# Transposing the normalised rows of twelve of sixteen x tiles with the DMA crossbar in place of TensorE

## The chip, the cores and the metric

The kernel runs on one core of one Trainium2 chip. The metric is the time of one execution on the device in microseconds; the median of several runs is compared. A profile is one further execution, taken by the hardware profiler.

## The reference, cut to what matters

```python
def reference(A_x, A_w_r, A_w_i, B_x, B_w_in, B_w_sp, B_b_sp, B_w_out):   # S = 2048, D = 576, Fh = 2304
    xn = layernorm(A_x)                      # over D
    s = irfft2(rfft2(xn) * (w_r + 1j * w_i)) # 2-D Fourier filter over S and D
    z = gelu(xn @ w_in)                      # D -> 2 Fh
    z1, z2 = z[..., :Fh], layernorm(z[..., Fh:])
    g = w_sp @ z2 + b_sp[:, None]            # mixes along S
    g = silu((z1 * g) @ w_out)
    return A_x + s * g
```

Everything that multiplies xn on TensorE, the first Fourier step along D and both halves of xn @ w_in, needs xn with D on the partitions: a transpose of each 128 rows.

## The kernel before

The 2048 rows are 16 tiles of 128 (MT = 16). A normalised row is laid out as KS = 5 blocks of 128 columns: four blocks of D, and a fifth that holds the 64 columns left over twice, so that the upper and the lower half of the partitions can each feed a half-height matmul.

**The first stage**, which the change touches, goes over the tiles. For tile m:

- ln1(m): VectorE takes mean and variance (L270, L274), GpSimd the reciprocal root (L261, L263).
- ln1_apply(m), L289: two VectorE operations (L293, L296) write the normalised row into XN[m % 3], one of three buffers.
- xpose(m), L300: five TensorE transposes into a PSUM tile pt of the pool psh (L304), and one ScalarE copy (L305) into xnT[:, m], which keeps all sixteen transposed tiles.
- p0_fold(m), L309: VectorE makes sums and differences of mirrored blocks (L311, L312) into one of four buffers FS.
- p0(m), L324, and p0_tail(m), L316: the first Fourier product, eight matmuls of 128 x 290 out of FS and two half-height ones out of the fifth block of xnT.
- p0_out(m), L332: ScalarE copies the product to bf16 (L334), GpSimd's queue stores it into the DRAM tensor Ad (L336).

In between, fill(1) emits a chunk of xn @ w_in: four full matmuls and a half-height one of 128 x 384 (L458), with GELU on ScalarE (L477). For the first 32 chunks these are of the second half of w_in.

The order is written out by hand: inside manual_schedule (L740) the queues of SP, TensorE and VectorE run in the order of the source; ScalarE and GpSimd are ordered by the framework's scheduler. Tiles 0, 1 and the start are written singly; the loop at L781 goes over m = 2 to 15. An even pass emits xpose(m + 1), p0_fold(m), ln1(m + 3), ln1_apply(m + 2), a chunk, p0(m), a chunk with the half-height matmuls of tiles m and m + 1 (p0_pair, L752). An odd pass emits p0_fold(m), ln1(m + 3), ln1_apply(m + 2), p0(m), p0_out(m), a chunk, xpose(m + 1), a chunk. So tile m + 2 is normalised in pass m and folded in pass m + 2.

SP's queue, in its order, first carries x (in four pieces), w_in for the second half, constants (CDSD, then G1, 1 MB, as c_g at L257), then MM (c_mm, L780), then the first two groups of w_in for the other half: load_win1 (L242), called in the passes m = 6 and m = 9 and made of two large loads (L232) and four small ones (L236). Each SP DMA completes on one of eight semaphores in turn, and waits until the DMA eight places ahead of it has completed on the same one. No SP DMA of this stretch waits for an engine, so they are issued as early as these waits allow, ahead of the passes in which they stand in the source.

After the loop: eleven chunks, then the further Fourier steps through DRAM (Ad, Bd, Ed, Yd) mixed with the rest of the chunks (to about 210 us), and then the product with w_sp, the gate and w_out (L617, L671). The slabs of w_sp are loaded with DMA transposes from DRAM on SP (L534).

Of the kernel before, what the change touches and what calls it, by code (L numbers as in the profile page):

```python
# [90 lines left out]
def kernel(  # L91
# [12 lines left out]
    nc = tc.nc  # L104
# [4 lines left out]
    MT = S // P  # L109
    KS = (D + P - 1) // P  # L110
# [57 lines left out]
    def reg(name, off, n):  # L168
        return AR[:, offs[name] + off: offs[name] + off + n]
# [15 lines left out]
    XN = [reg("XN", i * KS * P, KS * P) for i in range(3)]  # L185
# [7 lines left out]
    xnT = reg("XT", 0, MT * KS * P).rearrange("p (m k t) -> p m k t", m=MT, k=KS)  # L193
# [48 lines left out]
    def load_win1(g):  # L242
        fs = slice((g % (FT // WG)) * WG * P, (g % (FT // WG) + 1) * WG * P)
        wb = WIN1[g % 2]
        load_win(wb, fs)
# [36 lines left out]
    def ln1(m):  # L282
        ln1_stats(m)
        ln1_aggr(m)
# [4 lines left out]
    def ln1_apply(m):  # L289
        xn = XN[m % 3]  # L290
        mean, rs = ln1_of[m]
        xr = XC[m // 4][:, m % 4, :].rearrange("p (a d) -> p a d", a=2)
        nc.vector.tensor_scalar(out=xn[:, 0:4 * P].rearrange("p (b a i) -> p a b i", b=2, a=2),  # L293
                                in0=xr[:, :, 0:2 * P].rearrange("p a (b i) -> p a b i", b=2), scalar1=mean, scalar2=rs,
                                op0=ALU.subtract, op1=ALU.mult)
        nc.vector.tensor_scalar(out=xn[:, 4 * P:KS * P].rearrange("p (r a i) -> p r a i", r=2, a=2),  # L296
                                in0=xr[:, None, :, 2 * P:H2].to_broadcast((P, 2, 2, HT)), scalar1=mean, scalar2=rs,
                                op0=ALU.subtract, op1=ALU.mult)

    def xpose(m):  # L300
        xn = XN[m % 3]
        pt = psh.tile([P, KS, P], BF16, tag="h")
        for ks in range(KS):
            nc.tensor.transpose(pt[:, ks, :], xn[:, ks * P:(ks + 1) * P], ident[:])  # L304
        nc.scalar.activation(out=xnT[:, m, :, :], in_=pt[:], func=ACT.Identity)  # L305
# [3 lines left out]
    def p0_fold(m):  # L309
        xe, xo = xnT[:, m, 0:KS - 1:2, :], xnT[:, m, 1:KS - 1:2, :]  # L310
        nc.vector.tensor_tensor(out=FS[m % 4][:, 0, :, :], in0=xe, in1=xo, op=ALU.add)  # L311
        nc.vector.tensor_tensor(out=FS[m % 4][:, 1, :, :], in0=xe, in1=xo, op=ALU.subtract)  # L312
# [11 lines left out]
    def p0(m, start):  # L324
        if start:
            p0_ps[m] = psa.tile([P, 2, 512], F32, tag="a", name="pa")
        for par in range(2):
            for k in range(2):
                nc.tensor.matmul(p0_ps[m][:, par, 0:2 * LE], lhsT=FS[m % 4][:, par, k, :], rhs=CDSD[:, par, k, :],  # L329
                                 start=start and k == 0, stop=not start and k == 1, skip_group_check=True)  # L330

    def p0_out(m):  # L332
        sg = PST[m % 8].rearrange("p (c l) -> p c l", c=2)
        nc.scalar.activation(out=sg.rearrange("p c (l a) -> p a c l", a=2),  # L334
                             in_=p0_ps[m][:, :, 0:2 * LE].rearrange("p a (c l) -> p a c l", c=2), func=ACT.Identity)
        nc.gpsimd.dma_start(out=Adw[m], in_=sg[:, :, 0:L])  # L336
# [175 lines left out]
    def spend(pe, dve=0.0):  # L512
        load["pe"] += pe
        if dve:
            load["dve"] = max(load["dve"], load["pe"]) + dve
# [193 lines left out]
    def fill(n, lead=1.2, tails=None, ahead=None):  # L709
        for _ in range(n):  # L710
            i = place[0]
            place[0] += 1
            if i % 4 < 2:
                held.append(chunk(i))
                full(held[-1], True)
            if i % 4 == 1:
                if ahead:
                    ahead()
                done = held[:]
                held[:] = [chunk(i + 1), chunk(i + 2)]  # L720
                assert not tails or n == 1
                for r, c in enumerate(sorted(done + held, key=lambda c: c.wide)):
                    c.mm(KS - 1, slice(r % 2 * KT, (r % 2 + 1) * KT), c in held, c in done)
                if tails:
                    tails()
            elif i % 4 >= 2:
                done = [held.pop(0)]
                full(done[0], False)
            else:
                done = []  # L730
            for c in done:
                if c.wide == ZC:
                    z1_store(None, None)
                tick[0] += 1
                c.post()
            spend(0.82 if kinds[i] == "2" else 1.07)
            z2_stats(lead)

    SP, PE, DVE = mybir.EngineType.SP, mybir.EngineType.PE, mybir.EngineType.DVE
    with tc.manual_schedule(engines={SP, PE, DVE}):  # L740
# [11 lines left out]
        def p0_pair(m):  # L752
            p0_tail(m, False)
            p0_tail(m + 1, True)
            p0_out(m)

        ln1(0)
        ln1_stats(1, (0,))
        nc.vector.reciprocal(out=ln1_of[0][1], in_=ln1_of[0][1])
        ln1_apply(0)  # L760
        nc.scalar.activation(out=THF[:, 0:1], in_=ln1_of[0][1], func=ACT.Gelu_apprx_tanh)
        xpose(0)
# [3 lines left out]
        fill(1, 0)  # L766
        ln1(2)
        ln1_apply(1)
        p0_fold(0)
        ln1_apply(2)  # L770
        ln1(3)
        fill(1, 0, lambda: p0_pair(0), lambda: (xpose(1), p0(0, True), xpose(2)))
# [6 lines left out]
        fill(1, 0)  # L779
        nc.sync.dma_start(out=MM, in_=cd_mm.ap().rearrange("p (a k) -> p a k", a=3))  # L780
        for m in range(2, MT):  # L781
            if m % 2 == 0:
                xpose(m + 1)
            spend(0.78, 2.35 if m + 3 < MT else 0.6)
            p0_fold(m)
            if m + 3 < MT:
                ln1(m + 3)
            if m + 2 < MT:
                ln1_apply(m + 2)
            if m % 2 == 0:  # L790
                fill(1, 0)
                p0(m, True)
                fill(1, 0, lambda: p0_pair(m))
            else:
                p0(m, False)
                p0_out(m)
                fill(1, 0)
                if m + 1 < MT:
                    xpose(m + 1)
                fill(1, 0)  # L800
            if m in (6, 9):
                load_win1(m // 9)
# [119 lines left out]
```

## Time and profile before

| | us |
|---|---|
| median of 3 runs (lowest, highest) | 502.13 (502.05, 502.26) |
| the profiled execution, own time | 501.63 |
| its span | 499.9 |
| TensorE busy | 489.2 |
| VectorE busy | 342.6 |
| ScalarE busy | 169.4 |
| GpSimd busy | 210.8 |

The page's part 1 gives the busy time of each engine; PE is TensorE's matmuls, PEld its weight loads, DVE VectorE, ACT ScalarE, POOL GpSimd, SP the engine that only issues DMAs (its queue is SPq). The granted TensorE clock was 1.00 over the execution. A chain of waits is followed back from the last instruction to what released it; a timeline lists instructions with start, duration, engine, line, operation, tiles written and read, and in brackets the idle time before and what ended it. DMA issues list size and the median time from issue to landing. AR is one large SBUF tile that holds nearly all buffers, so XN, xnT, FS and the weights all appear under that name and are told apart by line and shape.

### The profile page before, as it was taken

The page shows a single profiled execution, that of the slowest core. Times are in us where ns is not written, and L with a number is a line of the kernel's source. Part 1 is how long each engine was busy: PE and PEld are TensorE (multiplying, and loading weights), DVE is VectorE, ACT ScalarE, POOL GpSimd, SP SyncE. Part 2 cuts the span into 40 slices and gives each one's busy share as a digit, 9 for nine tenths or more (in the row PEclk, how much of TensorE's full clock was granted, in tenths as well). Part 3 has the DMA queues.
Part 4 walks back from the last instruction along what each step waited for, and adds up shares of the span by engine and source line. Part 5 has one row for each costly group of instructions (what it writes and reads, how often), then busy time and mean ns, then how long its engine had stood idle before and what let it go on. Part 6 is the DMA issues. An engine that isn't in the chain of part 4 may idle for free.

```text
span 499.9 us, 9370 instructions
## 1 busy us (share of the span) xinstructions
PE 489.2 (98%) x3454; PEld 308.6 (62%) x3454; DVE 342.6 (69%) x746; ACT 169.4 (34%) x355; POOL 210.8 (42%) x281
## 2 busy tenths in 40 slices
PE   7999999999999999899999999999999999999996
PEld 2655454555556544466666677666666678888885
DVE  5776588898656798966565648856656547877734
ACT  4878777686778556200000011000000011000001
POOL 2664324434242684644535501455354301666600
PEclk9999999999999999999999999999999999999999
DMA  7951688988362999772112599021111863111202
GB/s 244 352 160 49 229 284 250 329 223 229 122 242 87 243 245 251 198 244 64 33 33 63 121 158 229 25 63 33 47 49 33 173 136 94 51 48 45 79 26 71
DMA packets 86766, 70.67 MB, mean 141 GB/s; under 512 B 39776, under 2 KB 79328, under 8 KB 86464
## 3 DMA queue, kind: packets, MB, share of 16 engines
q1 hardware_dynamic: 80480, 55.54, 42.1%
q0 software_dynamic: 5008, 13.71, 8.3%
q10 hardware_dynamic: 1232, 0.82, 0.6%
q8 instruction: 27, 0.44, 0.4%
q14 instruction: 19, 0.16, 0.1%
HBM read 40.40 MB, written 21.26 MB: 123 GB/s over the span
## 4 chain that ended last, share of the span: by engine, by line
PE 87%; ACT 5%; DVE 3%; DMA 2%; issue 1%; SPq 0%; ACTq 0%; DVEq 0%
PE pm L617 43%; PE po L671 13%; PE ph L554 13%; PE ph L458 12%; ACT AR L334 2%; PE pb L386 2%; PE pa L329 2%; DMA AR<-in_A_x_dram 1%; ACT Z_74 L477 1%; PE pa L428 1%; PE pa L374 1%; ACT AR L305 1%; ACT Z_74 L471 1%; DVE AR L540 1%; PE pa L350 1%
## 5 line engine op out<-in xcount | busy, mean ns | idle before, releaser
L617 PE MATMUL pm<-AR,Z_74 128*128 128x384 bf16 (+1 forms) x864 | 138.7, 308 | 0.0
L621 DVE TENSOR_TENSOR AR<-pm,AR 128x384 f32<-128x384 f32 (+3 forms) x162 | 82.4, 513 | 69.8 <-PE pm L617 66.5
L617 PEld LDWEIGHTS <-Z_74 128*128 128x128 bf16 x864 | 84.5, 98 | 40.6
L617 PE MATMUL pm<-AR 128*128 128x384 bf16 (+1 forms) x648 | 107.0, 308 | 2.2 <-DVE AR L621 1.5
L458 PE MATMUL ph<-AR 128*128 128x384 bf16 (+1 forms) x480 | 90.3, 327 | 1.5 <-ACT AR L305 0.9
L554 PE MATMUL ph<-AR 128*128 128x512 bf16 (+1 forms) x360 | 85.9, 379 | 0.0
L617 PEld LDWEIGHTS <-AR 128*128 128x128 bf16 x648 | 63.3, 98 | 33.2 <-issue 2.1
L631 ACT ACTIVATE AR<-pm 128x384 f32<-128x384 f32 (+1 forms) x27 | 12.3, 454 | 187.8 <-PE pm L617 187.8
L671 PE MATMUL po<-AR 128*128 128x288 bf16 x540 | 66.6, 286 | 0.0
L671 PEld LDWEIGHTS <-AR 128*128 128x128 bf16 x594 | 56.9, 98 | 13.9
L605 POOL TENSOR_TENSOR AR<-Z_74,AR 128x1024 bf16<-128x1024 bf16 x27 | 57.9, 2143 | 14.3 <-PE pm L617 13.4
L458 PEld LDWEIGHTS <-AR 128*128 128x128 bf16 (+1 forms) x480 | 39.9, 97 | 37.1 <-issue 15.2
L574 POOL DMA_DIRECT2D Z1d<-AR x55 | 32.0, 582 | 57.8 <-ACT AR L563 55.0
L632 POOL TENSOR_TENSOR AR<-AR 128x384 f32<-128x384 f32 (+1 forms) x27 | 23.3, 862 | 75.7 <-ACT AR L631 75.1
L554 PEld LDWEIGHTS <-AR 128*128 128x128 bf16 (+1 forms) x360 | 30.2, 97 | 28.1 <-issue 5.5
L563 ACT ACTIVATE AR<-ph 128x512 bf16<-128x512 f32 x72 | 42.1, 593 | 15.6 <-PE ph L554 15.4
L477 ACT ACTIVATE Z_74<-ph 128x384 bf16<-128x384 f32 x66 | 31.9, 501 | 24.5 <-PE ph L458 24.3
L674 ACT ACTIVATE TH<-po 128x576 f32<-128x576 f32 x15 | 9.8, 650 | 77.8 <-PE po L671 77.8
L635 POOL TENSOR_TENSOR AR<-AR 128x384 f32<-128x384 f32 (+1 forms) x27 | 30.5, 1128 | 11.5 <-DVE AR L621 11.5
L628 DVE TENSOR_TENSOR AR<-AR 128x384 bf16<-128x384 bf16 (+1 forms) x108 | 31.7, 335 | 0.9
L680 DVE SCALAR_TENSOR_TENSOR AR<-TH,po 128x576 bf16<-128x576 f32 x15 | 11.3, 754 | 30.0 <-ACT TH L674 29.9
L686 POOL DMA_DIRECT2D out_dram<-AR x12 | 6.6, 548 | 52.4 <-DVE AR L684 46.0
(185 smaller groups left out, 503.3 us busy)
## 6 DMA issues: line engine op xcount, KB each, us to landing
Z1d<-AR POOLq DMA_DIRECT2D x55, 128.0 KB, 4.0
AR<-Z1d SPq DMA_DIRECT2D x36, 192.0 KB, 3.0
AR<-in_A_x_dram SPq DMA_DIRECT2D x18, 144.0 KB, 2.9
AR<-in_B_w_out_dram SPq DMA_DIRECT2D x1, 2592.0 KB, 11.3
Ad<-AR POOLq DMA_DIRECT2D x16, 144.5 KB, 3.4
AR<-Ad SPq DMA_DIRECT2D x4, 578.0 KB, 6.0
AR<-in_A_w_r_dram SPq DMA_DIRECT2D x16, 144.5 KB, 4.4
AR<-in_A_w_i_dram SPq DMA_DIRECT2D x16, 144.5 KB, 3.9
```

Source lines behind the costliest of these rows:

```text
L458: nc.tensor.matmul(self.ph[:], lhsT=xnT[rows, self.m, ks, :], rhs=WIN2[rows, ks, n * ZC:(n + 1) * ZC], start=start, stop=stop)
L477: nc.scalar.activation(out=zc, in_=ph[:], func=ACT.Gelu_apprx_tanh)
L554: nc.tensor.matmul(self.ph[:].rearrange("p (a t) -> p a t", a=4), lhsT=wb[rows, ks, (fi % WG) * P:(fi % WG + 1) * P], rhs=xnT[rows, 4 * tq ...
L563: nc.scalar.activation(out=zs, in_=ph[:], func=ACT.Gelu_apprx_tanh)
L574: (nc.sync if place[0] > len(kinds) - 16 else nc.gpsimd).dma_start(out=d, in_=s_)
L605: nc.gpsimd.tensor_tensor(out=t, in0=zblk(p, 1, 0), in1=t2, op=ALU.subtract)
L617: nc.tensor.matmul(dst, lhsT=z[:, s, :], rhs=SLB[SA[name]][:, s, 0:nt], start=(s == 0 and not more), stop=(s == HM - 1), skip_group_check= ...
L621: nc.vector.tensor_tensor(out=out, in0=x, in1=y, op=ALU.add)
L628: nc.vector.tensor_tensor(out=o, in0=o, in1=zb[:, f, h, 0:nt], op=ALU.mult)
L632: nc.gpsimd.tensor_tensor(out=p1b, in0=p1, in1=B[1], op=ALU.add)
L635: nc.gpsimd.tensor_tensor(out=ux, in0=p1a, in1=B[0], op=ALU.add)
L671: nc.tensor.matmul(pv[:, hh, :], lhsT=U[:, fi, h, i * P:(i + 1) * P], rhs=WOUT[:, fi, c0 + hh * H2:c0 + hh * H2 + w // nh], start=(fi == 0 ...
```

## The change

A new function xpose_dma(m) issues one DMA on SP that transposes XN[m % 3], as five blocks of 128 x 128 in bf16 (160 KB), into xnT[:, m]. In the loop it follows ln1_apply(m + 2), for tile m + 2: tiles 4 to 15. The TensorE transposes of these tiles and their ScalarE copies go; tiles 0 to 3 keep theirs. On SP's queue the transposes of tiles 4 to 8 now stand between c_mm and load_win1(0), those of 9 to 11 between the two load_win1, those of 12 to 15 ahead of the first read of Ad. Each waits for VectorE's ln1_apply, and for the DMA eight places ahead. p0_fold of a tile and its half-height matmuls wait for its DMA.

```diff
+    def xpose_dma(m):
+        nc.sync.dma_start_transpose(out=xnT[:, m, :, :], in_=XN[m % 3].rearrange("p (k i) -> p k i", k=KS))
+
     def xpose(m):
         xn = XN[m % 3]
         pt = psh.tile([P, KS, P], BF16, tag="h")
...
         for m in range(2, MT):
-            if m % 2 == 0:
+            if m == 2:
                 xpose(m + 1)
             spend(0.78, 2.35 if m + 3 < MT else 0.6)
             p0_fold(m)
...
                 ln1(m + 3)
             if m + 2 < MT:
                 ln1_apply(m + 2)
+                xpose_dma(m + 2)
             if m % 2 == 0:
                 fill(1, 0)
                 p0(m, True)
...
                 p0(m, False)
                 p0_out(m)
                 fill(1, 0)
-                if m + 1 < MT:
-                    xpose(m + 1)
                 fill(1, 0)
```

In the changed kernel the lines after this function are three higher: L304, L305, L311, L334, L458 become L307, L308, L314, L337, L461, and the new DMA is L301.

## The prediction

> **What bounds the kernel now.** I read the page's engine shares first, then the chain of waits over 15 to 60 us (the stretch in which the x tiles are transposed), the timelines of VectorE and of SP's DMA queue there, and the DMA issues with their landing times. TensorE is the bound of the whole:
>
> ```profile
> PE 489.2 (98%) x3454; PEld 308.6 (62%) x3454; DVE 342.6 (69%) x746; ACT 169.4 (34%) x355; POOL 210.8 (42%) x281
> ```
>
> So after the stretch nothing has slack: a delay or a gain in it reaches the end whole. In the stretch one pair of tiles takes 5.20 us, each like the last. One round of the chain (start, us, what):
>
> ```profile
> 25.81 0.67 PE pa L329 x4
> 26.48 0.96 PE ph L458 x6
> 27.44 0.86 ACT Z_74 L477 x2
> 28.30 1.39 ACT AR L334 x2
> 29.69 0.34 ACT Z_74 L477
> 30.03 0.61 ACT AR L305
> 30.64 0.02 issue
> 30.66 0.30 DVE AR L311
> 30.96 0.05 issue
> 31.01 0.67 PE pa L329 x4
> ```
>
> It is a loop of latencies: TensorE's products, ScalarE's copies in order, last among them the copy of the next transpose (L305), the fold of that tile on VectorE (L311), TensorE again. TensorE waits in it only shortly: in its timeline four L458 matmuls take 0.65 us from start to next start (28.24 to 28.89), the last four before the fold start at 30.10, so 30.75 to 31.01 is idle, 0.26 us a round. VectorE waits longer:
>
> ```profile
> 25.46 0.29 DVE L311 TENSOR_TENSOR AR<-AR 128x256 bf16<-128x256 bf16 x1 [1.32 <-ACT AR L305]
> 26.84 0.37 DVE L293 TENSOR_SCALAR AR<-AR,mv_399,rs 128x512 bf16<-128x512 bf16 x1
> 27.13 0.31 DVE L296 TENSOR_SCALAR AR<-AR,mv_399,rs 128x128 bf16<-128x128 bf16 x1
> ```
>
> This is the fold of tile 6 and the normalisation of tile 8, which ends at 27.44, 1.98 us after the fold began; the fold of tile 8 begins at 30.66. A transposed tile has 30.66 - 27.44 = 3.22 us from normalised row to fold. The third view is the queue the transposes will join. SP's issues, and the landing times of what was issued from 17 to 24 us (last column, median us from issue to landing):
>
> ```profile
> 17.57 0.35 SPq L257 DMA_DIRECT2D AR<-c_g  x1
> 18.89 0.34 SPq L780 DMA_DIRECT2D AR<-c_mm  x1
> 20.17 0.97 SPq L232 DMA_DIRECT2D AR<-in_B_w_in_dram  x2
> ```
> ```profile
> DMA  9999999999899999999999999999969696997997
> ...
> AR<-c_g SPq DMA_DIRECT2D x1, 1024.0 KB, 9.5
> AR<-in_A_x_dram SPq DMA_DIRECT2D x1, 576.0 KB, 6.9
> ...
> AR<-in_B_w_in_dram SPq DMA_DIRECT2D x2, 192.0 KB, 7.9
> AR<-c_mm SPq DMA_DIRECT2D x1, 96.0 KB, 8.6
> ```
>
> The DMA engines are full, and 96 KB takes as long as what stands before it: c_mm lands at 18.89 + 8.6 = 27.5, right after c_g (17.57 + 9.5 = 27.1).
>
> **What the skill says.** The Trainium skill, "DMA: Bandwidth & Descriptors", section "Queues, rings and completion order": on each DMA engine descriptors are consumed in ring order, and SP owns one ring on each. The c_mm landing agrees. Same page, "DMA Transpose (X-bar)": the plain DMA transpose is issued from SP or ScalarE only, into SBUF; its rules ask for nothing beside ordinary DMAs. The trace has such transposes (of the slabs, from DRAM) between plain loads on SP. Same page, "Latency and other measured facts": 261 GB/s for a transpose on one kernel; this trace gives less (below), and its number is used. "TensorE: Matmul & The Clock Gate", "Part 1: The HAM clock gate": after an idle window of about 3.4 us TensorE runs at half clock until it has been busy for about as long. No run here shows it; the granted clock is 1.00 in every stretch I read.
>
> **The change part by part.**
>
> *Removed: twelve groups of five TensorE transposes (L304) and their ScalarE copies (L305).* The matmul rows overlap, so I take start to next start: 28.89 to 29.17 and 29.82 to 30.10, 0.28 us a group. Per pair 0.56 us of TensorE goes, and with the ScalarE copy out of the loop the 0.26 us of idle could go too: 5.20 - 0.82 = 4.38 us. Six pairs: at most 4.9 us. The twelve copies (0.77 us each) leave an engine with room and count only through that loop. This gain needs transposes that land in time.
>
> *Added: twelve transposes of 160 KB on SP, each waiting for its normalisation; what one takes.* The slab transposes are the nearest row: 256 KB each, 1.27 us of SP for one issue, landing, for the first of a group:
>
> ```profile
> AR<-in_B_w_sp_dram SPq DMA_TRANSPOSE x1, 3.7
> ```
> ```profile
> AR<-in_B_w_sp_dram SPq DMA_TRANSPOSE x1, 4.5
> ```
>
> (issued at 160.9 and 391.1 us). In 160 to 172 us SP's queue carried only six of them and was busy 71.3% of 16 engines: 12 x 0.713 / 6 = 1.43 us of all engines each, 183 GB/s. For five blocks in place of eight, 3/8 x 1.43 = 0.54 us less: 3.2 to 4.0 us. A transpose out of SBUF is not in the trace: a source nearer than DRAM could save some tenths (low end 2.9), and issuing it tile by tile from SBUF could cost more (high end 5.0). With the handovers VectorE to SP and DMA to VectorE I take 3.6 us from normalised row to fold.
>
> *The first transposes.* Tile 4 is normalised early, but its DMA stands in SP's order just behind c_mm, and each DMA waits for the semaphore of the one eight before it. That is the place of the first L232 load of before: issued at 20.17, landing 7.9 us later, at 28.1. The transpose holds less data but at the slower rate, so I take 28.3. The fold of tile 4 was at 20.26: 8.0 us of stall, and it is TensorE's too, since p0(4) stands next in its fixed order and only matmuls already ahead of it can run. Bounds: 7.2 (landing with c_mm) and 9. Tile 5 follows in the ring about 1 us later and its fold is due 1.98 us after tile 4's: nothing more. A stall this long should drop the clock as the skill has it; 3.4 us of half speed costs 1.7 us of TensorE, but afterwards TensorE has slack in each round (next step), so I add nothing; if that cover is missing it costs 1.7.
>
> *The rounds after it.* The loop is now fold(m), 1.98 us of VectorE to the end of normalising m+2, the DMA, fold(m+2): 1.98 + 3.6 = 5.58 us a pair, above TensorE's 4.38. The odd tiles' VectorE work (again 1.98) lies inside the wait. Five rounds from fold 4 to fold 14: 5 x (5.58 - 5.20) = +1.9 us. With 2.9 us it is 5 x (4.88 - 5.20) = -1.6, with 5.0 it is +8.9.
>
> *Moved: two loads of the first w_in half.* load_win1(0) now stands on SP behind the transpose of tile 8, load_win1(1) behind that of tile 11, and tiles 9 and 12 behind these loads. Each load is six DMAs, 0.97 us for the two large and 1.9 us for the four small where nothing holds them (at 174.30 and 175.30 us): 2.9 us. With about 0.9 us for the transpose ahead (5/8 of 1.27 and a little), SP is free 3.8 us after tile 8's issue, and tile 9 was ready after 1.98: 1.8 us late. The first delays the odd tiles, and the even ones by 0.3; the second delays the even ones by 1.8 more: together 2.1 us. The weights themselves are needed only in the first L554 matmul near 52 us. GpSimd's queue: the reciprocal roots and Ad stores keep their order nearly; the roots are ready over a microsecond before their use. Nothing.
>
> *Sum.* 8.0 + 1.9 + 2.1 = +12.0 us. The profiled execution took 501.63 (span 499.9), so 513.6; it lies 0.5 below the median of the runs, 502.13, so the median becomes 514.1.
>
> **Rivals.**
>
> *TensorE becomes the only bound (faster).* If a transpose goes from normalised row to fold in at most 4.38 - 1.98 = 2.4 us and isn't held by the loads, all 4.9 us are won: 497.2. For it: TensorE's 98%, and VectorE's idle 1.3 us. Against: no transpose in the trace landed under 3.7, and c_mm's 8.6.
>
> *The loads don't hold the first transposes* (the crossbar's work passes them). Then only the cadence and w_in cost: 1.9 + 2.1 = +4.0, 506.1. Against: ring order.
>
> *Out of SBUF the transpose is much slower* (many small writes, an issue per tile): 6.0 us gives 8.0 + 5 x 2.78 + 2.1 = +24.0, 526.1. For it: nothing in the trace has an SBUF source.
>
> *The change does nothing that can be measured*: the first stall cancelled by gains elsewhere; that needs a landing near 2.4 us and a stall under 5.
>
> **How the numbers follow.** Forecast 0.68 (its own range 508 to 521), transposes that pass the loads 0.12, very slow transposes 0.13, TensorE bound 0.05, no change 0.02. The range 506 to 521 takes in the first two and leaves out the rest, 0.2. Low end of the forecast: 7.2 - 1.6 and little for w_in; high end: 8 + 8.9 + 2. Slower by over 0.2% (about what a measurement of this kernel can tell from no change): 0.68 + 0.12 + 0.13 = 0.93; faster 0.05; same 0.02.
>
> **What would show it.** The first L301 transpose is issued near 20 us and lands near 28; the first fold that waits for a DMA starts near 28.3, TensorE idle about 8 us before it, with a lower clock in that slice. Then rounds of 5.6 us set by DMA to VectorE, no ScalarE in the chain; tiles 9 and 12 late behind L232 and L236 on SP. From the last fold on, all as before, 12 us later. It is wrong if the transposes land before c_mm, if one takes under 2.9 or over 5 us in the quiet stretch after 34 us, or if the rounds are at 4.4.

## The result and the profile after

| | before | after |
|---|---|---|
| median, us (lowest, highest) | 502.09 (502.00, 502.26) | 514.59 (512.91, 515.45) |
| ratio, 95% interval | | 1.0244 [1.0217, 1.0272] |
| the profiled execution, own time | 501.63 | 515.05 |
| its span | 499.9 | 513.3 |
| last product p0(15) starts at | 48.55 | 61.71 |

The kernel became 12.5 us slower; the forecast was +12.0. Each run below was measured side by side with the kernel before, whose median then lay between 501.5 and 502.3 us; gains over it are counted from that median. The span grew by 13.4 us in the profiled execution, and 13.2 of that is there when the last first-stage product starts: the loss lies in the stretch that the change touches.

First the page's engine shares after the change, and the head of its last chain (shares by engine):

```profile
PE 488.0 (95%) x3394; PEld 305.9 (60%) x3394; DVE 342.5 (67%) x746; ACT 163.1 (32%) x343; POOL 209.0 (41%) x281
...
PE 80%; DMA 12%; DVE 4%; ACT 2%; issue 1%; ACTq 0%; POOL 0%; SPq 0%; DVEq 0%; POOLq 0%
```

TensorE has 60 matmuls and about 1.2 us less work, and is busy for a smaller share of a longer span; transfers now hold 12% of the chain (2% before). The chain of waits over 18 to 63 us (start, us, what) shows where. ScalarE is gone from it, and a DMA from AR to AR, the transpose, stands in its place:

```profile
21.02 7.88 DMA AR<-AR
...
28.92 0.29 DVE AR L314
...
30.68 0.22 DVE AR L296
...
30.93 2.75 DMA AR<-AR
...
44.78 4.29 DMA AR<-AR
...
49.18 4.75 DMA AR<-AR
```

The first transpose takes 7.88 us, a later one 2.75, two others over 4. The row of the first one was ready at 16.36, but SP issued it at 21.02, when the DMA eight places ahead of it, a load of w_in, had landed (20.94). Issues from 17 to 19 us and from 19 to 20.5 us show what was then on its way in front of it on SP's queue:

```profile
AR<-c_g SPq DMA_DIRECT2D x1, 1024.0 KB, 9.8
```
```profile
AR<-c_mm SPq DMA_DIRECT2D x1, 96.0 KB, 9.2
```

Issued at 18.43 and 19.55, they land at 28.2 and 28.7, and the transpose at 28.9. The wait shows also in VectorE's timeline, folds of tiles 4, 12, 14 and 15 (in brackets the wait before each and what ended it):

```profile
28.92 0.29 DVE L314 TENSOR_TENSOR AR<-AR 128x256 bf16<-128x256 bf16 x1 [10.19 <-DMA AR<-AR]
...
54.02 0.29 DVE L314 TENSOR_TENSOR AR<-AR 128x256 bf16<-128x256 bf16 x1 [2.89 <-DMA AR<-AR]
...
58.70 0.29 DVE L314 TENSOR_TENSOR AR<-AR 128x256 bf16<-128x256 bf16 x1 [1.21 <-DMA AR<-AR]
61.36 0.29 DVE L314 TENSOR_TENSOR AR<-AR 128x256 bf16<-128x256 bf16 x1 [2.17 <-DMA AR<-AR]
```

Tile 4's fold was at 20.26 before, tile 14's at 46.27, tile 15's at 47.26. So tile 4 is 28.92 - 20.26 = 8.66 us late; from fold 4 to fold 14 it takes 29.78 us in place of 26.01; fold 15 follows fold 14 after 2.66 us in place of 0.99. The even folds stand at 28.92, 33.77, 39.02, 45.83, 54.02 and 58.70: rounds of 4.85, 5.25, 6.81, 8.19 and 4.68 us, which were all 5.20.

TensorE's timeline has its wait at the same place, and a table of the two stretches gives the granted clock (in each row: us, TensorE busy, then PEld, DVE, ACT and POOL, then the clock, the DMA share, GB/s):

```profile
29.27 1.15 PE L332 MATMUL pa<-AR 128*128 128x290 bf16 x4 [9.43 <-DVE AR L314]
```
```profile
20.30:28.90 8.60, 0.00 (x0) 0.00 (x0) 0.00 (x0) 0.00 (x0) 0.09 (x1) 0.62 1.08 284
28.90:33.80 4.90, 4.53 (x24) 2.24 (x25) 3.82 (x15) 1.64 (x4) 1.99 (x4) 0.63 0.19 35
```

No matmul ran in the first of these stretches, 8.6 of the 9.43 us that TensorE waited, while the DMA engines were full (share 1.08). The four matmuls after it took 1.15 us, and 0.67 us in the kernel before.

Last, SP's queue around the two loads of w_in. A row of several DMAs shows how long they kept SP, with their waits:

```profile
35.76 1.20 SPq L301 DMA_TRANSPOSE AR<-AR  x1
37.01 1.10 SPq L232 DMA_DIRECT2D AR<-in_B_w_in_dram  x2
38.16 1.86 SPq L236 DMA_DIRECT2D AR<-in_B_w_in_dram  x4
40.11 5.87 SPq L301 DMA_TRANSPOSE AR<-AR  x3
```

Tile 9's transpose is issued at 40.11, because the six loads occupy SP until 40.02; its normalised row was ready at 37.61 (the end of its L296 in VectorE's timeline), 2.5 us earlier. Before tile 12 the same happens for 1.4 us (47.80 to 49.18).

### The profile page after: what moved, and what is told of

Same layout as the page of the kernel before. It is cut to its first block, busy times and chain, and to the rows that moved or that the text cites. A ratio compares the mean times of both kernels' runs of the same rounds, so it can differ in the third digit from the quotient of the medians.

```text
span 513.3 us, 9263 instructions
## 1 busy us (share of the span) xinstructions
PE 488.0 (95%) x3394; PEld 305.9 (60%) x3394; DVE 342.5 (67%) x746; ACT 163.1 (32%) x343; POOL 209.0 (41%) x281
## 2 busy tenths in 40 slices
DMA packets 94829, 72.62 MB, mean 141 GB/s; under 512 B 47840, under 2 KB 87392, under 8 KB 94528
## 4 chain that ended last, share of the span: by engine, by line
PE 80%; DMA 12%; DVE 4%; ACT 2%; issue 1%; ACTq 0%; POOL 0%; SPq 0%; DVEq 0%; POOLq 0%
PE pm L620 41%; PE po L674 13%; PE ph L557 12%; PE ph L461 9%; DMA AR<-AR 6%; DMA AR<-in_B_w_in_dram 4%; PE pb L389 1%; DMA Z1d<-AR 1%; PE pa L431 1%; DMA AR<-in_A_w_i_dram 1%; PE pa L377 1%; ACT Z_74 L474 1%; PE pa L405 1%; PE pa L353 0%; PE pl L674 0%
## 5 line engine op out<-in xcount | busy, mean ns | idle before, releaser
L461 PE MATMUL ph<-AR 128*128 128x384 bf16 (+1 forms) x480 | 89.3, 330 | 1.4 <-ACT AR L308 0.9
L461 PEld LDWEIGHTS <-AR 128*128 128x128 bf16 (+1 forms) x480 | 40.7, 97 | 39.1 <-issue 15.6
L683 DVE SCALAR_TENSOR_TENSOR AR<-TH,po 128x576 bf16<-128x576 f32 x15 | 11.3, 754 | 30.0 <-ACT TH L677 29.9
L379 DVE TENSOR_TENSOR AR<-pa,AR 128x578 bf16<-128x578 f32 x32 | 22.9, 753 | 8.3 <-PE pa L377 6.6
## 6 DMA issues: line engine op xcount, KB each, us to landing
Ad<-AR POOLq DMA_DIRECT2D x16, 144.5 KB, 3.9
AR<-in_A_w_r_dram SPq DMA_DIRECT2D x16, 144.5 KB, 3.5
AR<-in_A_w_i_dram SPq DMA_DIRECT2D x16, 144.5 KB, 3.8
```

Source lines behind the costliest of these rows:

```text
L379: nc.vector.tensor_tensor(out=tt[:, c, :, :], in0=pa[:, :, 0:L], in1=wt[:, c, hh % 4:hh % 4 + 2, :], op=ALU.mult)
L461: nc.tensor.matmul(self.ph[:], lhsT=xnT[rows, self.m, ks, :], rhs=WIN2[rows, ks, n * ZC:(n + 1) * ZC], start=start, stop=stop)
```

## The experiments

My theory at this point had four parts: the 1 MB load on its way holds the first transpose; SP's loads of w_in hold tiles 9 and 12; transposes land in 2.6 to 2.8 us when alone, and in 4 us or more when a store of a product to Ad (L339, on GpSimd's queue) is under way; the removal of TensorE's work is worth about 5 us. The rivals stand with each run. Each edit below is against the changed kernel.

**1. The constants loaded late.**

```diff
-    nc.sync.dma_start(out=G1, in_=cd_g1.ap().rearrange("p (s k) -> p s k", s=N2))
-        nc.sync.dma_start(out=MM, in_=cd_mm.ap().rearrange("p (a k) -> p a k", a=3))
...
+        nc.sync.dma_start(out=G1, in_=cd_g1.ap().rearrange("p (s k) -> p s k", s=N2))
+        nc.sync.dma_start(out=MM, in_=cd_mm.ap().rearrange("p (a k) -> p a k", a=3))
```

Both stand behind the last transpose now.

> The changed kernel with the loads of G1 (1 MB) and MM (96 KB) moved on SP from ahead of the first transpose to behind the last. Theory, ring order: the transpose of tile 4 lands behind the last x load (24.65 us in the changed kernel's profile) at about 25.3 and no longer at 28.9, the first fold waits 3.6 us less, the rounds after it stay: 514.6 - 3.6 = 511.0 (509.5 to 512.5). Rival, a transpose out of SBUF is slow by itself while other queues are busy: tile 4 still lands near 28.9, 514.6.

Measured: 512.30 us (511.00 to 514.17), ratio 1.0215 [1.0187, 1.0244]. Tile 4's transpose is issued at 17.29 and lands at 24.2, 0.8 us after the 576 KB of x issued before it (16.74 + 6.72 = 23.46). Again it lands with the load ahead of it, so the rival (slow by itself) falls; fold 4 is 4.7 us earlier than in the changed kernel. From fold 4 to fold 14 it still takes 29.9 us. The stall and the rounds are two separate costs. The total gained only 2.3 us by the medians, 3.8 us by the spans: the transpose of tile 15, now beside a store and the moved 1 MB load, takes 4.63 us, and the last p0 starts only 3.6 us earlier.

**2. A lead of three tiles**, so that VectorE normalises tile m + 3 in pass m and a transpose has one more pass to land.

```diff
+        ln1(5)
+        ln1_apply(4)
+        xpose_dma(4)
...
+            if m + 4 < MT:
+                ln1(m + 4)
             if m + 3 < MT:
-                ln1(m + 3)
-            if m + 2 < MT:
-                ln1_apply(m + 2)
-                xpose_dma(m + 2)
+                ln1_apply(m + 3)
+                xpose_dma(m + 3)
```

> The changed kernel with each tile normalised and its transpose issued one pass earlier (three passes ahead of its fold, where it was two). Theory, latency: three passes now have to cover 1.98 us and the transpose's 2.6 to 4.7 us, that is at most 4.5 us a pair, so the five rounds from the fold of tile 4 to that of tile 14 fall from 29.8 us to TensorE's own 4.4 each, 22, plus up to 1.7 of slow clock after the first stall, which stays; the fold of tile 15 is no longer late (0.9): 514.6 - 7 = 507.6 (506 to 509.5). Rival, the crossbar's or SP's throughput (1.2 us an issue, contention) sets the rounds: they stay above 5 us a pair, 512 or more.

Measured: 519.39 us (518.51 to 520.62), ratio 1.0359 [1.0339, 1.0379]: a miss in the total. In the stretch the theory held for three rounds of five: from tile 6 to tile 12 a round takes 4.37 us. The first one, at a low clock, takes 6.89 and the last 5.00, so the five take 25.0 us where 22 to 23.7 were expected. The last p0 starts at 57.00 in place of 61.71, 4.7 us earlier. The gain is lost after the loop. TensorE's timeline there, and GpSimd's:

```profile
75.32 0.64 PE L353 MATMUL pa<-AR 128*128 128x289 bf16 x2 [6.78 <-DMA AR<-Ad]
```
```profile
65.64 0.26 POOL L261 TENSOR_SCALAR ve<-mv,one 128x1 f32<-128x1 f32 x1 [10.63 <-DVE mv L504]
...
66.51 1.48 POOL L339 DMA_DIRECT2D Ad<-AR  x2
```

The scheduler, which orders GpSimd, put a root of the second normalisation ahead of the last two stores to Ad. The root waits for statistics of VectorE (L504) until 65.64, so the stores leave at 66.51, 8.8 us after the last product left TensorE (57.67), and TensorE waits 6.78 us for Ad to be read back. A new order on one engine moved a store on another that nobody had edited.

**3. The same with the stores of tiles 14 and 15 on SP's queue**, which keeps the order of the source.

```diff
-        nc.gpsimd.dma_start(out=Adw[m], in_=sg[:, :, 0:L])
+        (nc.sync if m >= 14 else nc.gpsimd).dma_start(out=Adw[m], in_=sg[:, :, 0:L])
```

> The kernel with transposes three passes ahead, and in it the Ad stores of tiles 14 and 15 issued on SP's queue, ahead of the read of Ad, in place of GpSimd's. Theory: there the two stores stood behind a root for z2 (L261) that waits for 8.3 us of VectorE's statistics, and TensorE waited 6.8 us for Ad; with that gone the kernel is late only by what the loop is: last p0 at 57.0 us against 48.55 before, 502.1 + 8.5 = 510.6 (509 to 512). Rival, something else after the loop is late: it stays at 517 or more.

Measured: 512.27 us (511.75 to 513.20), ratio 1.0179 [1.0145, 1.0214]. The wait for Ad is gone, which confirms the cause given for run 2. The total lies 0.3 us above the range that I had given. Fold 4 waits for its transpose until 30.57, 10.3 us later than before the change; p0(4) starts at 30.92 and p0(6) at 37.86, then a round takes 4.37 us up to tile 12, and the last p0 starts at 57.64, 9.1 us later than before. With a lead of three, what is left of the change's cost is the first stall and a slow round after it (the last round, 4.73 us, is 0.4 over 4.37).

**4. The loads of w_in after the last transpose.**

```diff
-            if m in (6, 9):
-                load_win1(m // 9)
+            if m == 13:
+                load_win1(0)
+                load_win1(1)
```

> The changed kernel with both load_win1 groups moved on SP behind the transpose of tile 15. Theory one, these loads make the two long rounds (fold 8 to 10 is 6.8 us, 10 to 12 is 8.2, quiet rounds 4.85): both fall to about 5, 514.6 - 5 = 509.6. Theory two, they only hold SP (tiles 9 and 12 issued 1.1 and 1.4 us late) and the long landings of 4.3 us come from the Ad stores on GpSimd's queue: 514.6 - 2.1 = 512.5, and landings of 4 us and more remain. Rival, SP's order costs nothing: 514.6.

Measured: 523.45 us (521.23 to 524.92), ratio 1.0431 [1.0398, 1.0463], a miss. As in run 2, the last store to Ad leaves behind a waiting root (at 71.27), and TensorE waits 5.09 us for it. Before that, the stretch from fold 4 to fold 14 takes 26.86 us in place of 29.78, but tile 15's transpose, now beside the loads and four stores, takes 5.6 us and delays its fold to 61.57, so that nothing is won by the end of the loop (fold 4 itself came 1.3 us later in this execution, at 30.20). Tile 12's takes 5.3 us with stores beside it and no w_in: the loads aren't the only cause of the long transposes.

**5. The stores to Ad after the loop, still on GpSimd's queue**, with sixteen staging buffers in place of eight.

```diff
-        nc.gpsimd.dma_start(out=Adw[m], in_=sg[:, :, 0:L])
+        ad_later.append((m, sg))
...
+        for m, sg in ad_later:
+            nc.gpsimd.dma_start(out=Adw[m], in_=sg[:, :, 0:L])
```

> The changed kernel with all sixteen stores of the first product (Ad, GpSimd's queue) issued only after the loop, from sixteen staging buffers in place of eight. The end of the stage comes later by that, so only the stretch up to the fold of tile 14 is compared. Theory, the stores and the transposes slow each other: every transpose from tile 6 on lands in 2.6 to 3.0 us, those of tiles 10 to 13 and 15 too (4.3, 4.3, 4.7, 4.3 and 3.7 in the changed kernel), and fold 4 to fold 14 takes about 26.5 us in place of 29.8. Rival, the w_in loads on the same queue make them long: the landings of tiles 10 to 13 stay above 4 us.

Measured: 513.12 us in one execution. The test says nothing: the scheduler put the stores back among the rounds (at 40.17, 43.97, 47.11, 50.47 and 56.36), and the transposes beside them took 3.7 to 4.9 us as in the changed kernel.

**6. The same stores on SP's queue**, where the order of the source holds.

```diff
-            nc.gpsimd.dma_start(out=Adw[m], in_=sg[:, :, 0:L])
+            nc.sync.dma_start(out=Adw[m], in_=sg[:, :, 0:L])
```

(This one is against run 5.)

> The changed kernel with sixteen staging buffers for the channel mixing's results and all sixteen Ad stores issued on SP's own queue after the last transpose, so that no store to Ad is under way beside a transpose. Theory (a store to Ad and a transpose slow each other): every transpose from tile 6 on lands 2.6 to 3.0 us after its issue, and from the fold of tile 4 to that of tile 14 it is about 26.5 us instead of 29.8; what is left above 26.0 is the lateness of tiles 9 and 12 behind the loads of w_in. Rival (the long landings come from the w_in loads): tiles 10 to 13 still land 4 us or more after their issue and the stretch stays at 29 us or more. The total is made later by the sixteen stores that now come together at the end of the stage; it is not compared.

Measured: every transpose from tile 6 on lands 2.6 or 2.7 us after its issue, tile 12's, beside w_in, 3.0. The one execution took 524.33 us, which is not compared. DMA issues at 44.2 us of this run and from 44.8 to 46 us of the changed kernel, both tile 11, with w_in loads issued 1.3 us behind it in both:

```profile
AR<-AR SPq DMA_TRANSPOSE x1, 2.6
```
```profile
Ad<-AR POOLq DMA_DIRECT2D x1, 144.5 KB, 4.0
AR<-AR SPq DMA_TRANSPOSE x1, 4.3
```

So the stores to Ad on GpSimd's queue made the long transposes, and the rival (w_in) falls for these. Whether the store itself does it or the queue that it is on, no run separates. The packets say where the time goes. A transpose consists of 640 packets of 256 bytes and 32 of 4 bytes. Packets of SP's queue in 1.05 us of this run (45.30 to 46.35) and of the changed kernel (45.90 to 46.95):

```profile
q1 hardware_dynamic: 672, 0.16, 79.8%
```
```profile
q1 hardware_dynamic: 640, 0.16, 79.0%
```

The data of tile 11 moved as fast beside the store as without it. Only the 32 small packets were missing, and the transpose landed 2.2 us after its data had moved (0.5 us in this run), at 49.07, beside the store's landing at 49.30. Tile 15's is the same (data in 0.95 us, landing 1.6 us after it, the store's 0.2 us later); in tiles 10, 12 and 13 the data took 1.5 to 2.1 us, and the landing came 1.5 us after it. Nor is it enough that both are under way. In all runs with stores on GpSimd's queue, 33 transposes issued after 28 us had a store issued between 0.2 us before and 0.6 us after them, and every one of them took 3.1 us or more; but four in runs 4, 10 and 11, whose next store was issued 0.7 to 0.8 us after them, landed in 2.6 us. What holds the landing back stays open.

The stretch from fold 4 to fold 14 takes 28.12 us, where I had expected 26.5. Its rounds are 4.77, 4.67, 6.22, 7.79 and 4.67 us. Three of them are quiet; the two with a load of w_in are 1.5 and 3.1 us longer, 4.6 together. Tile 9 is issued 2.5 us after it is ready (37.05 to 39.54), as in the changed kernel; tile 12 now 2.7 us (46.05 to 48.78) in place of 1.4, since with faster transposes its row is ready sooner.

**7. No transposes at all.** The loop without the DMAs. It leaves out the transposes of tiles 4 to 15 and reads the transposed tiles 0 to 3 in their place.

```diff
-                xpose_dma(m + 2)
...
-        xe, xo = xnT[:, m, 0:KS - 1:2, :], xnT[:, m, 1:KS - 1:2, :]
+        xe, xo = xnT[:, m % 4, 0:KS - 1:2, :], xnT[:, m % 4, 1:KS - 1:2, :]
...
```

> Left out: tiles 4 to 15 are not transposed at all, and everything that reads a transposed tile reads that of tile 0 to 3 in its place (same shapes). It shows what the removal alone is worth. Theory: 0.56 us of TensorE and 0.26 us of idle go per pair, rounds of 4.38 us, 502.1 - 4.9 = 497.2 (496.5 to 498). Rival, the ScalarE chain without the copies or VectorE (3.8 us busy a pair) still sets the round: near 4.8 us, 499.5. Rival, the removal is worth nothing: 502.1.

Measured: 499.64 us (499.35 to 500.51), ratio 0.9963 [0.9948, 0.9978]. All rounds take 4.37 us and the last p0 starts 5.1 us earlier than before the change, but only 1.9 us arrive at the end (501.54 beside it). The total is near the first rival's 499.5, but not for its reason, since no round takes 4.8 us. After the loop TensorE waits 0.9 us for Ad (the last stores leave at 47.69, again behind a root) and 1.5 us for ScalarE's copies at L355.

**8. The same, with the last two stores on SP** as in run 3.

> Left out: the transposes of tiles 4 to 15, as in the other kernel without them (tiles 0 to 3 are read in their place); the Ad stores of tiles 14 and 15 are on SP's queue. Theory: the loop ended 5.1 us earlier there (last p0 at 43.44 us, 48.55 before) and 3 us of that were lost waiting for Ad; now all of it arrives: 502.1 - 5.1 = 497.0 (496.3 to 498). Rival, another wait behind it takes the gain: 499 to 500.

Measured: 496.97 us (496.82 to 497.49), ratio 0.9880 [0.9852, 0.9909]. This is the ceiling of the idea, if transposes cost nothing anywhere: 5.3 us by the medians (502.31 beside it), 4.6 us by the profiled executions (501.63 and 496.99). In the profile 4.5 us of it are there when the last p0 starts (44.06). TensorE was busy without a gap over 14 to 44 us, 30.00 of 30 us.

**9. The transposes on ScalarE's queue.** Is it the order on SP's queue that held the first transpose, or the DMA engines' backlog?

```diff
-        nc.sync.dma_start_transpose(out=xnT[:, m, :, :], in_=XN[m % 3].rearrange("p (k i) -> p k i", k=KS))
+        nc.scalar.dma_start_transpose(out=xnT[:, m, :, :], in_=XN[m % 3].rearrange("p (k i) -> p k i", k=KS))
```

> The changed kernel with the twelve transposes issued on ScalarE's queue, which has its own ring, in place of SP's; each still waits for its apply, now in ScalarE's order. Only the landing of tile 4's transpose is read: if the ring's order alone held it (theory), it lands 3 to 4 us after its issue although the 1 MB mixing matrix is still under way on SP's ring, at about 24 us; if the DMA engines were the limit whatever the ring (rival), it lands at 27 us or later. The total is not compared, since ScalarE stands still in each wait.

Measured (one execution, 515.38 us, not compared): tile 4's transpose is issued at 17.68 and lands at 24.1, after 6.4 us, which fits neither: SP's issue of the 1 MB load had itself slipped to 24.53, so tile 4 didn't meet it. Tile 6's did. It was issued on ScalarE's queue at 26.12, just after the constants; the DMA issues from 24.5 to 26.2 us:

```profile
AR<-c_g SPq DMA_DIRECT2D x1, 1024.0 KB, 8.2
AR<-in_B_w_in_dram SPq DMA_DIRECT2D x1, 192.0 KB, 8.3
...
AR<-AR ACTq DMA_TRANSPOSE x1, 8.6
```

The transpose takes 8.6 us on a queue of its own, and lands at 34.7, 0.8 us after the w_in load issued before it (25.56 + 8.3 = 33.9). The packets by queue (packets, MB, share of the 16 engines; q1 is SP's, q10 ScalarE's) from 26.2 to 28, 30 to 32, 32 to 33.9 and 33.9 to 34.8 us:

```profile
q1 hardware_dynamic: 397, 0.47, 96.0%
```
```profile
q1 hardware_dynamic: 202, 0.49, 75.1%
q10 hardware_dynamic: 166, 0.04, 18.2%
```
```profile
q1 hardware_dynamic: 525, 0.38, 70.2%
q10 hardware_dynamic: 526, 0.13, 35.9%
```
```profile
q10 hardware_dynamic: 652, 0.16, 104.4%
```

From 28 to 30 us SP's queue is alone as well, at 97.6%: for almost 4 us after the issue began, and for more than 2 us after ScalarE was done with it (27.82), ScalarE's queue moves nothing. A queue of its own didn't spare this transpose the wait for loads that were already on their way. The Trainium skill, "DMA: Bandwidth & Descriptors", section "Queues, rings and completion order", says that each engine takes turns between the queues that have work, packet by packet. From 32 to 33.9 us the trace agrees, with 525 packets of one queue and 526 of the other; before 30 us ScalarE's queue had no turn at all. What holds its first packets back I didn't settle.

**10. TensorE for tiles 4 to 7, the crossbar from tile 8 on**, with a lead of three, the loads of w_in in pass 12, behind the last transpose, and the last two stores on SP.

```diff
-            if m == 2:
+            if m % 2 == 0 and m < 7:
                 xpose(m + 1)
...
-                ln1_apply(m + 2)
-                xpose_dma(m + 2)
+                ln1_apply(m + 3)
+                if m + 3 >= 8:
+                    xpose_dma(m + 3)
...
+                if m < 7:
+                    xpose(m + 1)
...
-            if m in (6, 9):
-                load_win1(m // 9)
+            if m == 12:
+                load_win1(0)
+                load_win1(1)
```

> Tiles 4 to 7 by TensorE as before, while the DMA queues are full; tiles 8 to 15 by DMA, three passes ahead of the fold; w_in behind the last transpose; the Ad stores of tiles 14 and 15 on SP. Theory: no first stall, four pairs at 4.4 us in place of 5.2: 502.1 - 3.3 = 498.8 (498 to 500.5). Rival, landings of 5 us beside Ad stores still make rounds long, or the first DMA transposes still queue behind the constants: 501 or more.

Measured: 501.78 us, ratio 0.9975 [0.9958, 0.9991] to the kernel before: 3 us short of the forecast. There is no stall; rounds take about 4.4 us from 27.15 us on, and the last p0 starts 1.9 us earlier than before, of which 0.5 arrives (502.31 beside it). The early rounds had grown: p0(6) starts 1.3 us later than before (27.15 for 25.81).

**11. The same, with the old lead of two for the tiles before 8.** Run 10 also normalises tile 4 ahead of the loop, as run 2 does; this one doesn't, and in the loop it has:

```diff
-            if m + 3 < MT:
-                ln1(m + 3)
-            if m + 2 < MT:
-                ln1_apply(m + 2)
-                xpose_dma(m + 2)
+            for n in ((m + 2,) if m < 5 else (m + 2, m + 3) if m == 5 else (m + 3,)):
+                if n + 1 < MT:
+                    ln1(n + 1)
+                if n < MT:
+                    ln1_apply(n)
+                    if n >= 8:
+                        xpose_dma(n)
```

> The version with TensorE transposes for tiles 4 to 7, the crossbar for tiles 8 to 15 three tiles ahead, the w_in loads after tile 12 and the last two Ad stores on SP's queue, now with the tiles before 8 at the lead of two that they had, so that the early rounds do not grow. Theory: three to four rounds at 4.37 us in place of 5.20 and nothing lost early give 498.5 to 499.5 us. Rival (the gain in this stage is given back at 67 to 70 us, where the second stage's own stores are waited for): about 501.5 us, no faster than the version before it.

Measured: 501.21 us (498.32 to 503.82, 22 executions), before beside it 502.12 (501.04 to 504.91, 26), ratio 0.9972 [0.9955, 0.9988]. The last p0 starts at 45.79, 2.8 us earlier than before, and 0.9 us of it arrives. In the profiled execution, one of the slower ones (503.58), TensorE's waits that the kernel before doesn't have are these (us in total, times, longest):

```profile
PE pm L620 <- DVE AR L624: 2.3, 1, 2.3
...
PE pa L353 <- ACT AR L355: 1.1, 1, 1.1
...
PE pb L389 <- DVE AR L379: 0.7, 1, 0.7
...
PE pa L353 <- DMA AR<-in_A_w_r_dram: 0.5, 1, 0.5
```

The kernel before has 1.5 us in the first (there L617 and L621), and none of the other three; together they are 3.1 us more. TensorE's clock was also at half for a while (mean 0.57 from 210 to 214 us, just after the longest of these waits), by estimate (1 - 0.57) x 4 = 1.7 us more. The two are about the 4.7 us that this execution lost after the loop (2.8 earlier at the last p0, 503.58 - 501.63 = 1.95 later at the end). This version is faster than the kernel before by 0.3%: less than its stretch gained. The rival's total came true, its place only in part, since 1.6 of the 3.1 us are waited at 68 to 70 us. That the gain went there is read from one trace; no run takes these waits away.

## Why the prediction was right, point by point

| step | predicted, us | profiled, us |
|---|---|---|
| fold of tile 4 late | 8.0 | 8.66 |
| fold 4 to fold 14, cadence and w_in | 1.9 + 2.1 = 4.0 | 29.78 - 26.01 = 3.77 |
| from fold 14 to the last product | 0 | (61.71 - 58.70) - (48.55 - 46.27) = 0.73 |
| all after it | 0 | 13.4 - 13.16 = 0.24 |
| sum | 12.0 | 13.4 |

*The first transpose* was right, place and size: it landed at 28.9 where 28.3 was forecast, and TensorE stood for it. Runs 1, 3 and 10 show that it is two thirds of the loss: it shrinks when the loads ahead go, it is what stays with a lead of three, and it is gone when tiles 4 to 7 keep TensorE. The stores to Ad beside it are not its cause: in run 6, without them, tile 4's transpose still took 7.5 us. The reason may be too narrow. "Stands in SP's order just behind c_mm" names one ring; in run 9 a transpose issued just behind the constants on another queue landed as late (8.6 us). That is one transpose, and why it waited is open.

*The clock* fell, as the step on "TensorE: Matmul & The Clock Gate", section "Part 1: The HAM clock gate", of the Trainium skill had it: a mean of 0.62 in the idle stretch, and matmuls at 1.15 us for 0.67 after it. It was hidden, as argued: the first round, mostly at half clock (0.50 from 29.3 to 32.5 us), took 4.85 us, near the 4.67 of quiet rounds at full speed, because the loop went over VectorE and the transfer. Where TensorE is the bound the cover is gone: in run 3 the first round after the stall takes 37.86 - 30.92 = 6.94 us in place of 4.37, 2.6 us more, where I had put 1.7 on it. The clock stayed at 0.50 from 30.92 to 36.30, which is 5.4 us of dense matmuls and not the 3.4 taken from that section; for this run the measurement decides. In the changed kernel it was 3.2, near that figure.

*The rounds* came out right as a sum (3.77 us for 4.0), from terms that were wrong: that was luck. The forecast had one duration, 3.6 us from normalised row to fold, and so even rounds of 5.58. There are two durations. A transpose alone lands in 2.6 us, below the low end of 2.9 that I gave it; with VectorE's 2.0 us that makes rounds of 4.7, and five of them, 23.5 us, are 2.5 us less than before. Beside stores to Ad five transposes of this kernel took 3.7 to 4.8 us and one, tile 8's, 3.2. The stretch with stores and no w_in in it (run 4) took 26.86, 3.3 us over the quiet 23.5; with w_in and no stores (run 6) 28.12, 4.6 over; with both 29.78, 6.3 over. That is less than 3.3 + 4.6: the waits overlap, as with tile 12, which SP holds 2.7 us without the stores and 1.4 with them. Quiet transposes saved 2.5 and these two cost 6.3: +3.8. By the forecast's own test ("if one takes under 2.9 or over 5 us in the quiet stretch after 34 us") the cost of the transpose was wrong, and nearly cancelled by what stood beside it.

*The w_in loads* held tiles 9 and 12 as described, by 2.5 and 1.4 us where 1.8 was forecast for each, but their price was taken too low: 0.3 + 1.8 = 2.1 us for the rounds, and run 6, without the stores, has 1.5 + 3.1 = 4.6. From tile 8's issue SP is held 4.35 us (35.76 to 40.11) and not 3.8 (the transpose alone keeps it 1.20 us, where I had taken about 0.9 from 5/8 of 1.27), which explains tile 9. And the shorter the round, the less of an odd tile's lateness VectorE can take up, as it still has 1.9 us of work between an odd fold and the next even one: by the forecast's rounds 5.58 - 2 x 1.98 = 1.6 us are free, in quiet rounds of 4.68 only about 0.9. So tile 9, 2.5 us late, delays fold 10 by 1.5 in run 6. That is worked out from the timeline, not tested by a run of its own. Tile 12 was late already, behind a long transpose, and without one it is 2.7 (run 6). So the price of the loads depends on that of the transposes: the two terms can't be added.

*The stores to Ad* were the missing term. The forecast looked at GpSimd's queue for its order only ("Nothing"), not for what its stores do to a transpose beside them. In the changed kernel the order indeed changed nothing that TensorE waits for; in runs 2, 4 and 7 it cost 6.8, 5.1 and 0.9 us, so "nothing" was true of one order and not of the neighbouring ones. (That the roots are ready over a microsecond before their use also fails for tile 15: VectorE waits 0.46 us for its root, before the change and after.)

*Tile 15* was also missed: its transpose, issued at 57.52, took 3.75 us beside a store issued at 57.88, and no later round hides the last tile. Of its 1.67 us 0.94 came back, since the last product now starts 0.35 us after its fold and not 1.29.

*The removal* was sized well: rounds of 4.37 us (forecast 4.38) and, in run 8, 4.6 to 5.3 us in all (forecast at most 4.9). It is never the bound in the changed kernel, since each of its rounds waits for a transfer.

*The reach.* "A delay or a gain in it reaches the end whole" held for the delay: 13.16 us at the last product, 13.4 at the end. For gains it failed in three of four runs: of 5.1 us in run 7, 1.9 in run 10 and 2.8 in run 11, 1.9, 0.5 and 0.9 us arrived. In run 7 it was waits after the loop, and with two stores moved (run 8) the gain arrived whole.

*The rivals.* TensorE as the only bound needs a transpose of at most 2.4 us; it takes 2.6 at best, and with a lead of three the rounds do get to TensorE's 4.37 (run 3). That the loads don't hold the first transposes and that the transposes are very slow both fall by the first chain above, and that the change does nothing falls by the result.

## What to carry to other kernels

Moving work from a busy engine to the DMA engines is worth what the engine saves only if each transfer has room to land: here that meant a lead of three tiles in place of two, and starting when the initial loads have nearly drained (run 11's first transpose is issued at 25.44, and c_mm lands at 28.8). Neither a place further ahead on the queue (run 1) nor another queue (run 9) passed the backlog. Price a new transfer twice, alone and beside the stores and loads that run with it, and don't add the waits of terms that share one loop. And when an edit changes when buffers and results come, look again at the order that a scheduler gives to every other engine: a store behind a waiting instruction of another stage cost more here than the edited step had won (run 2: 6.8 us for 4.7).

## What the runs showed of the hardware

- A transpose of 160 KB from SBUF to SBUF keeps SP 1.20 us and lands 2.6 us after its issue when little else moves. A transpose of 256 KB from DRAM keeps SP 1.27 us, hardly more for 1.6 times the bytes (the sources differ too).
- Beside stores of 144.5 KB from SBUF to DRAM on GpSimd's queue, in the stretch after the initial loads, it takes 3.1 to 5.7 us where a store is issued from 0.2 us before to 0.6 us after it (33 transposes of nine kernels), but 2.6 in four cases where the next store was issued 0.7 to 0.8 us after it. The stores took 2.9 to 5.0 us in the changed kernel there, 2.6 to 3.5 before the change. In the changed kernel two of the five longest moved their data in 0.95 us as without a store, and landed 1.6 and 2.2 us after it, within 0.25 us of the store's landing.
- It moves as small packets: the page counts 47,840 packets under 512 bytes after and 39,776 before, 8,064 more for twelve transposes, 672 each: 640 of 256 bytes, which are the 160 KB, and 32 of 4 bytes.
- Behind loads of over 1 MB it lands within 1 us of them, 7.9 us after its issue on the same queue and 8.6 on another.
- In a stretch of 8.6 us without a matmul TensorE's granted clock was 0.62 in the mean (0.50 from 22.3 us on), and it stayed at 0.50 for 3.2 us of matmuls after it. In run 3 it stayed at 0.50 for 5.4 us.
